# Converting float64 weights in four passes in place of six, under a written-out order, in a delta-rule attention and low-rank mixer kernel

## The chip, the core and the metric

The kernel runs on one core of a Trainium2 chip. The metric is the device time of one execution in microseconds (us). Five engines run side by side, each through its own instruction queue in program order: PE (TensorE, matmuls and transposes into PSUM), DVE (VectorE), ACT (ScalarE), POOL (GpSimd) and SP (SyncE, which here issues transfers only). An instruction waits in its queue until the results that it needs are there, and holds everything behind it in that queue.

## The reference

```python
# attention: B=4, H=8, S=768, D=48
k_n = k / (norm(k) + 1e-6)
for t in range(S):
    y[:, :, t] = q_t @ state
    state = state + beta_t * outer(k_t, v_t - state^T k_t)
x = y as (B, S, 384)
# mixer: U (768,32), V (32,768), w_ch1 (384,1536), w_ch2 (1536,384)
u = x + ((x^T @ U) @ V)^T
out = u + relu(u @ w_ch1) @ w_ch2
```

U, V and the two channel matrices are made with float64 arithmetic and reach the kernel as float64: two 32-bit words an element. q, k, v and beta are float32.

## The kernel before

**The work.** The delta rule is cut into chunks of 64 tokens. A *unit* is one batch entry and half of its sequence (six chunks, all eight heads), so there are eight units, n = 0 to 7. For each unit the kernel loads k, q and v (L518), transposes k and q on PE (L633, copied out by ACT at L647), forms the products of keys (L660), lays their diagonal blocks out on DVE with a long transpose (L736), takes the norms (sqrt on ACT, L580), and inverts the 32x32 blocks on DVE by substitution, column by column (L745 and L751, a serial chain of up to 62 instructions). A second long transpose (L758) brings the result back, and small matmuls join the blocks (L801 to L862, with copies on ACT at L806, L849, L868, L880). Then the recurrence over chunks runs: PE, then DVE (L1022), PE, then DVE (L1047), with the outputs copied to X on ACT (L908). For each batch entry the mixer follows: `front` (L1335 to L1381: the product with U, with V, and a transpose), `channels` (L1438, the first channel matrix, Relu on ACT at L1403) and `narrow` (L1553, the second one in seven products, summed into X on DVE at L1478). The last batch entry's first channel matrix uses L1238 instead.

**The weights.** There are 14 slices, i = 0 to 13: U (192 elements in each of 128 partitions), V, six slices of w_ch1 and six of w_ch2 (768 elements in each partition). SP (POOL for U) issues their transfers as pairs of 32-bit words (L1119) into three rooms: part of X, a tile `wide`, and part of `hs`; by turns 0 1 0 1 2 0 1 2 0 1 0 1 0 1. A room is loaded again when its slice is `freed`. DVE and ACT make float32 of the words: DVE cuts out the exponent (L1142) and the upper mantissa (L1148) of the high word, adds the low word scaled by 2^-32 (L1154); ACT turns the exponent field into a power of two with a Relu (L1127); DVE puts the sign on (L1160) and multiplies mantissa by power into the weight tile (L1170). `freed` follows L1160. `front` needs U and V, `channels` y needs slice 2+y, `narrow` needs the slices from 8 on and sums of them (L1077).

**The order.** Nothing is ordered by hand in the loops. Every piece of work is a Python generator that yields `op(engine, cost, ...)` before each instruction and `need(...)` for what must come first. `run()` is a list scheduler: it keeps an estimated clock for each engine, and among the pieces that could start soon takes the one with the lowest *place*, a priority from the text table `PLACES`. What comes out is one fixed instruction order for each engine, and it is this order that the chip sees. PSUM is handed out in four pairs of banks (`take`, `give`) in the same order.

Of the kernel before, what the change touches and what calls it, by code (L numbers as in the profile page):

```python
# [10 lines left out]
U32 = mybir.dt.uint32  # L11
ALU = mybir.AluOpType
# [14 lines left out]
def kernel(  # L27
# [60 lines left out]
    asked, missing, awaited, woken, quads = {}, {}, {}, [], set()  # L88
# [11 lines left out]
    def op(  # L100
        engine, cost, mode=None, take=None, give=(), lat=None, rush=None, words=0, port=None, flow=None,
        after=(),
    ):
        return dict(
            after=after,
            flow=cost * 0.95 if flow is None else flow,
            e=engine, cost=cost, mode=mode, take=take, give=give, words=words + 0.4,
            port=engine == "pool" if port is None else port,
            rush=bool(give) if rush is None else rush, lat=LAT[engine] if lat is None else lat,
        )  # L110
# [31 lines left out]
    PLACES = """  # L142
    add_up b0 i0 79; add_up b0 i1 13.98; add_up b0 i2 2.35; add_up b1 i0 40.18; add_up b1 i1 36.03
    add_up b1 i2 41.5; add_up b2 i0 77.22; add_up b2 i1 83.5; add_up b2 i2 138.32; add_up b3 i0 49.5
    add_up b3 i1 70.77; add_up b3 i2 2.5; blocks n0 2.5; blocks n1 56.67; blocks n2 -4.99; blocks n4 112
    blocks n5 123.28; blocks n7 190.8; both -10; channels b0 i0 e1 50.01; channels b0 i0 e2 94.8
    channels b0 i0 e3 -11; channels b0 i0 e4 53; channels b0 i0 e5 48.96; channels b0 i1 e2 82.12
    channels b0 i1 e4 1.27; channels b0 i1 e5 7.7; channels b0 i2 e0 93.45; channels b0 i2 e1 -29.76
    channels b0 i2 e2 41; channels b0 i2 e3 54.83; channels b0 i2 e4 220.13; channels b0 i2 e5 120.58
    channels b1 i0 e0 95.14; channels b1 i0 e1 90.59; channels b1 i0 e2 2.6; channels b1 i0 e3 20.5  # L150
    channels b1 i0 e5 75.93; channels b1 i1 e1 82.72; channels b1 i1 e3 38.5; channels b1 i1 e4 95.89
    channels b1 i1 e5 84.94; channels b1 i2 e1 -0.77; channels b1 i2 e2 88.03; channels b1 i2 e3 2.65
    channels b1 i2 e4 106.63; channels b1 i2 e5 105.76; channels b2 i0 e0 98.76; channels b2 i0 e1 100
    channels b2 i0 e3 103.94; channels b2 i0 e4 54.62; channels b2 i0 e5 101.37; channels b2 i1 e0 71.97
    channels b2 i1 e1 110.54; channels b2 i1 e2 -17.79; channels b2 i1 e4 38.5; channels b2 i1 e5 83.8
    channels b2 i2 e0 79.5; channels b2 i2 e1 148.8; channels b2 i2 e2 23.18; channels b2 i2 e3 74.5
    channels b2 i2 e4 94.46; channels b2 i2 e5 96.7; diagonals n0 h0 42.32; diagonals n0 h1 70.57
    diagonals n1 h0 2.5; diagonals n1 h1 76.19; diagonals n2 h0 18.79; diagonals n2 h1 98.94
    diagonals n3 h0 78.08; diagonals n3 h1 69; diagonals n4 h0 67; diagonals n4 h1 21.77; diagonals n5 h0 31.5
    diagonals n5 h1 8.5; diagonals n6 h0 40.59; diagonals n6 h1 104; diagonals n7 h0 8.5; diagonals n7 h1 74.99  # L160
    first 126.7; first_of_last 96.5; front b0 i0 94.5; front b0 i2 73.04; front b1 i0 80.34; front b1 i1 76.11
    front b1 i2 123.31; front b2 i0 66.93; front b2 i1 98.32; front b2 i2 -8.5; front b3 i1 101; front b3 i2 34.14
    gather b0 i0 h0 c0 42.82; gather b0 i0 h1 c0 104.34; gather b0 i0 h1 c1 36.58; gather b0 i1 h0 c0 67.77
    gather b0 i1 h0 c1 63; gather b0 i1 h1 c0 88; gather b0 i1 h1 c1 -32.01; gather b0 i2 h0 c0 87.83
    gather b0 i2 h0 c1 38; gather b0 i2 h1 c0 151.77; gather b0 i2 h1 c1 56.81; gather b1 i0 h0 c0 -21.78
    gather b1 i0 h1 c1 69.02; gather b1 i1 h0 c0 112.22; gather b1 i1 h0 c1 3; gather b1 i1 h1 c1 4.54
    gather b1 i2 h0 c0 58.39; gather b1 i2 h0 c1 -1; gather b1 i2 h1 c0 21.95; gather b1 i2 h1 c1 32
    gather b2 i0 h0 c0 7.28; gather b2 i0 h0 c1 76.31; gather b2 i0 h1 c1 62.25; gather b2 i1 h1 c0 53.05
    gather b2 i1 h1 c1 98.26; gather b2 i2 h0 c0 26; gather b2 i2 h1 c0 69.29; gather b2 i2 h1 c1 68.5
    gather b3 i0 h0 c1 -14.78; gather b3 i0 h1 c0 115; gather b3 i0 h1 c1 80.5; gather b3 i1 h0 c0 41.85  # L170
    gather b3 i1 h0 c1 33.5; gather b3 i1 h1 c0 -6.5; gather b3 i1 h1 c1 102; gather b3 i2 h0 c0 75.5
    gather b3 i2 h1 c0 6.38; gather b3 i2 h1 c1 -23.64; grams n0 i1 32.5; grams n1 i0 53.5; grams n1 i1 110.77
    grams n2 i0 20; grams n2 i1 17; grams n3 i0 28.59; grams n3 i1 9.78; grams n4 i0 77.18; grams n5 i0 131.89
    grams n5 i1 107.96; grams n6 i1 -2.5; grams n7 i0 111.34; grams n7 i1 62.06; joins n0 h0 2.01
# [125 lines left out]
    def start_of(i, s):  # L300
        e, was = s["e"], last.get(i)
        at = max(was[1] if was and was[0] == e else ready[i], clock[e])
        if s["port"]:
            at = max(at, clock["port"])
# [1327 lines left out]
```

## Time and profile before

| | us |
|---|---|
| runs | 614.04, 616.64, 616.75 |
| median | 616.64 |
| span of the profiled execution (first to last instruction) | 611.9 |
| PE busy in the span | 574.0 |
| DVE busy | 417.7 |
| ACT busy | 235.0 |
| POOL busy | 97.9 |

The profile records one execution, and its span is the only time listed for it; the median run is 4.7 us longer than that span. Busy times of PE are those of pipelined matmuls, so an engine that reads as fully busy is not at its peak. The profile also gives the granted clock of TensorE, as a share of full speed, in each stretch of time. Shares are averages over the span; what a change in one stage is worth is read from that stage.

### The profile page before, as it was taken

What the parts mean: (1) busy time and instruction counts of PE and PEld (TensorE: products, weight loads), DVE (VectorE), ACT (ScalarE), POOL (GpSimd) and SP (SyncE); (2) the same over time, 40 slices, a digit from 0 to 9 for tenths busy, and PEclk for the clock granted to TensorE, in tenths of its full rate; (3) what the DMA queues carried; (4) which work ended last, traced back from release to release, by engine and by line L of the source; (5) the groups of instructions that cost most, each with busy time, mean ns of one, the idle gap of its engine ahead of it and who ended that gap; (6) DMA issues with size and microseconds to landing.
All of it is one profiled execution on the core that took longest, in us unless ns stands there. A gap on an engine that the chain in (4) does not pass through costs nothing.

```text
span 611.9 us, 23481 instructions
## 1 busy us (share of the span) xinstructions
PE 574.0 (94%) x10548; PEld 493.7 (81%) x10548; DVE 417.7 (68%) x1000; ACT 235.0 (38%) x462; POOL 97.9 (16%) x169
## 2 busy tenths in 40 slices
PE   3697968899999999999999999999999999999997
PEld 3596867688889888789898988789889868656997
DVE  4999998998989328998896068898872135232542
ACT  2575665446322553245124451354243221344000
POOL 9221112611141104101003214010100000000000
PEclk9767575999999999999999999999999999999999
DMA  9721659920152104300002315100200000000000
GB/s 153 145 48 56 209 173 188 181 64 4 43 107 38 47 4 80 72 14 3 29 0 51 78 42 93 36 1 3 67 3 2 29 3 1 26 0 1 16 37 27
DMA packets 63845, 33.28 MB, mean 54 GB/s; under 512 B 50816, under 2 KB 61824, under 8 KB 63744
## 3 DMA queue, kind: packets, MB, share of 16 engines
q1 hardware_dynamic: 56800, 23.21, 17.6%
q0 software_dynamic: 5344, 8.27, 6.4%
q8 instruction: 83, 1.36, 0.9%
q10 hardware_dynamic: 1600, 0.30, 0.3%
q14 instruction: 18, 0.15, 0.1%
HBM read 27.03 MB, written 4.72 MB: 52 GB/s over the span
## 4 chain that ended last, share of the span: by engine, by line
PE 78%; DVE 13%; ACT 2%; issue 2%; DVEq 0%; ACTq 0%
PE P L1553 27%; PE P L1438 23%; PE P L1238 7%; PE P L660 2%; PE P L1009 2%; PE P L633 2%; PE P L924 2%; PE P L1037 1%; PE P L938 1%; DVE prod L745 1%; DVE xt L751 1%; PE P L960 1%; PE P L971 1%; PE P L1378 1%; PE P L1335 1%
## 5 line engine op out<-in xcount | busy, mean ns | idle before, releaser
L1438 PE MATMUL P<-ut,w_sb 128*128 128x256 f32 x648 | 152.5, 386 | 0.0
L1438 PEld LDWEIGHTS P<-ut,w_sb 128*128 128x128 f32 x648 | 119.0, 190 | 18.9 <-issue 1.8
L1553 PE MATMUL P<-w_sb,hs 128*128 128x192 f32 x540 | 94.6, 330 | 0.2 <-ACT hs L1403 0.2
L1553 PEld LDWEIGHTS P<-w_sb,hs 128*128 128x128 f32 x540 | 87.5, 190 | 3.6 <-issue 1.2
L1478 DVE TENSOR_TENSOR X<-X,P 128x192 f32<-128x192 f32 x84 | 29.5, 351 | 59.6 <-PE P L1553 59.0
L751 DVE TENSOR_TENSOR xt<-xt,prod 128x112 f32<-128x112 f32 (+21 forms) x200 | 64.6, 323 | 6.9
L745 DVE TENSOR_TENSOR prod<-gs,xt 128x112 f32<-128x112 f32 (+21 forms) x200 | 64.1, 320 | 4.8
L1403 ACT ACTIVATE hs<-P 128x512 f32<-128x512 f32 x54 | 32.3, 598 | 85.5 <-PE P L1438 74.4
L908 ACT COPY X<-P 64x192 f32<-64x192 f32 x96 | 30.1, 314 | 63.1 <-PE P L938 62.1
L1553 PE MATMUL P<-w_sb,S 128*128 128x192 f32 x288 | 50.7, 330 | 0.0
L1553 PEld LDWEIGHTS P<-w_sb,S 128*128 128x128 f32 x288 | 46.6, 190 | 1.2 <-DVE X L1478 0.6
L633 PE MATMUL P<-ident,slot 128*128 128x128 f32 x192 | 30.5, 313 | 15.9 <-DMA slot<-in_k_dram 10.3
L633 PEld LDWEIGHTS P<-ident,slot 128*128 128x128 f32 x192 | 25.8, 162 | 18.2 <-issue 10.9
L647 ACT COPY slot<-P 128x768 f32<-128x768 f32 x30 | 23.1, 802 | 45.0 <-PE P L633 44.8
L518 POOL DMA_DIRECT2D slot<-in_k_dram x44 | 28.9, 664 | 50.7 <-PE P L1037 50.1
L880 ACT COPY slot<-zz 32x384 f32<-32x384 f32 x64 | 32.3, 508 | 8.7 <-DVE zz L758 6.5
L518 POOL DMA_DIRECT2D slot<-in_v_dram x32 | 21.0, 663 | 90.5 <-PE P L633 89.6
L660 PE MATMUL P<-slot 48*64 48x64 f32 x1536 | 32.3, 240 | 2.2 <-ACT slot L647 2.2
L1238 PE MATMUL P<-slot,w_sb 128*128 128x384 f32 x96 | 33.3, 486 | 0.0
L1022 DVE TENSOR_TENSOR z<-slot,P 128x192 f32<-128x192 f32 x44 | 15.5, 352 | 25.6 <-PE P L1009 25.1
L660 PEld LDWEIGHTS P<-slot 48*64 48x64 f32 x1536 | 29.3, 153 | 4.3 <-ACT slot L647 3.2
L1553 PE MATMUL P<-w_sb,slot 128*128 128x192 f32 x180 | 30.6, 327 | 0.9 <-DVE X L1478 0.9
(143 smaller groups left out, 889.5 us busy)
## 6 DMA issues: line engine op xcount, KB each, us to landing
out_dram<-X SPq DMA_DIRECT2D x22, 192.0 KB, 1.8
X<-in_moe_w_ch_dram SPq DMA_DIRECT2D x10, 384.0 KB, 4.5
wide<-in_moe_w_ch_dram SPq DMA_DIRECT2D x10, 384.0 KB, 4.5
slot<-in_k_dram SPq DMA_DIRECT2D x48, 72.0 KB, 5.0
slot<-in_k_dram POOLq DMA_DIRECT2D x44, 72.0 KB, 5.0
slot<-in_q_dram POOLq DMA_DIRECT2D x32, 72.0 KB, 4.8
slot<-in_q_dram SPq DMA_DIRECT2D x32, 72.0 KB, 5.4
slot<-in_v_dram SPq DMA_DIRECT2D x32, 72.0 KB, 3.3
```

Of the source, the lines that this page charges most:

```text
L518: queue.dma_start(out=t[half(1 - g if name == "z" else g), :, to, 0:D], in_=src[b, 4 * g + s, hf * UC * L : (hf + 1) * UC * L, :].rearrang ...
L633: nc.tensor.transpose(p_t[:, c // 3, c % 3], t[:, c, 2 * j : 2 * j + 2].rearrange("p s d -> p (s d)"), ident,)
L660: nc.tensor.matmul(p_g[half(g ^ (par * i)), par, c], kq[rows, c, j, 0, half(g)], kq[rows, c, j, i, half(g)], start=True, stop=True,)
L745: nc.vector.tensor_tensor(out=prod, in0=gb[:, :, j : j + 1, j + 1 :].to_broadcast([128, split, m, w]), in1=xb[:, :, 0:m, j : j + 1].to_bro ...
L751: nc.vector.tensor_tensor(out=xb[:, :, 0:m, j + 1 :], in0=xb[:, :, 0:m, j + 1 :], in1=prod, op=ALU.subtract,)
L880: nc.scalar.copy(pg[quarter(i), :, at, :, a : a + BK], cut(zc, h)[quarter(i)].rearrange("p r (c j) t -> p r c j t", j=2),)
L908: nc.scalar.copy(x[half(c % 2), c // 2, 4 * D * g : 4 * D * (g + 1)].rearrange("p (j r d) -> p r j d", r=2, d=D), states(p_y)[half(g)],)
L1238: nc.tensor.matmul(to, w, t, start=start, stop=stop, skip_group_check=True)
L1403: nc.scalar.activation(hs[:, fs[0] : fs[1] + 1 : fs[1] - fs[0]], p_f, ACTF.Relu)
L1438: nc.tensor.matmul(p_f[:, x], w(x, t), ut[:, t], start=(t == 0), stop=(t == KT - 1))
L1478: nc.vector.tensor_tensor(out=to, in0=to, in1=p, op=ALU.add)
L1553: nc.tensor.matmul(to, of[0], of[1], start=of[2], stop=of[3], skip_group_check=True)
```

## The change

Two things change together.

**The conversion.** ACT now reads the high words where they landed, as if they were float32, and multiplies them by 2^-112 into one of two scratch tiles (even and odd slices). DVE shifts the result left by three bits into the weight tile, puts the sign of the high word on, and adds the low word, scaled by 2^-29 and rounded, to the lower 16-bit half of each element in place. So a slice takes one ACT and three DVE instructions where it took one and five, and ACT's comes first. ACT's instruction waits for the transfer, and `freed` follows the last DVE instruction.

**The order.** `PLACES` and the scheduler go. A table `ORDER` lists, for 2,139 steps, which generator goes on next; `run()` follows it. The costs in `op(...)` no longer decide anything. Some waits are added that any order has to keep (for instance, a store of an output row waits until all four of its sums are in). PSUM banks go to the longest-free pair. No matmul is added or removed.

```diff
-    PLACES = """
-    add_up b0 i0 79; add_up b0 i1 13.98; add_up b0 i2 2.35; add_up b1 i0 40.18; add_up b1 i1 36.03
...
+    ORDER = """
...
     def run():
-        stall, forms = {}, {}
-        while waits or woken:
...
+        wake()
+        for y in range(len(ORDER)):
+            i = ORDER[y]
+            s, got = waits[i], None
+            s = s[0] if isinstance(s, tuple) else s
             if s["take"]:
...
-        uppers, powers = room[:, 2 * WIDE :], exponents
+        scaled = [t.bitcast(FP32) for t in (room[:, 2 * WIDE :], exponents)]
...
-        def raised(i, power):
-            cost = 0.16 + size(i) * 0.001
-            yield op("act", cost)
-            nc.scalar.activation(
-                power, power, ACTF.Relu, bias=bias_e, scale=2.0 ** 23
-            )
-            emitted(("raised", i))
+        def raised(i):
+            yield need(("wide", i), ("shifted", i - 2))
+            yield op("act", act(size(i)))
+            high = landed[i][:, :, 1].bitcast(FP32)
+            nc.scalar.mul(shape(i, scaled[i % 2][:, 0 : size(i)]), shape(i, high), 2.0 ** -112)
+            emitted(("raised", i), 0.06)
...
-            nc.vector.tensor_scalar(
-                out=power, in0=h, scalar1=20, scalar2=0x7FF,
-                op0=ALU.logical_shift_right, op1=ALU.bitwise_and,
-            )
-            begin(raised(i, power), 39)
-            nc.vector.tensor_scalar(
-                out=upper, in0=h, scalar1=0x000FFFFF, scalar2=0x00100000,
-                op0=ALU.bitwise_and, op1=ALU.bitwise_or,
+            nc.vector.tensor_single_scalar(
+                out=bits, in_=shape(i, scaled[i % 2][:, 0:n]).bitcast(I32), scalar=3,
+                op=ALU.logical_shift_left,
             )
-            mant = upper.bitcast(FP32)
             nc.vector.scalar_tensor_tensor(
-                out=mant, in0=low, scalar=2.0 ** -32, in1=upper,
-                op0=ALU.mult, op1=ALU.add,
-            )
-            yield need(("raised", i))
-            nc.vector.scalar_tensor_tensor(
-                out=power, in0=h, scalar=-(1 << 31), in1=power,
+                out=bits, in0=h, scalar=-(1 << 31), in1=bits,
                 op0=ALU.bitwise_and, op1=ALU.bitwise_or,
             )
-            emitted(("freed", i))
+            halves_of = dst.bitcast(U16)
+            tail = halves_of[..., 0::2]
             nc.vector.scalar_tensor_tensor(
-                out=dst, in0=mant, scalar=2.0 ** -20, in1=power, op0=ALU.mult, op1=ALU.mult
+                out=tail, in0=low.bitcast(U32), scalar=2.0 ** -29, in1=tail,
+                op0=ALU.mult, op1=ALU.add,
             )
+            emitted(("freed", i))
             emitted(("weights", i), 0.1)
```

What the written-out order does to the queues, as far as the prediction speaks of it. SP's first four transfers are half of unit 0's k (before, they were unit 1's, and unit 0's came fifth to eighth). U's transfer is POOL's first (before, it came after 14 others), and U's conversion stands among the first products of unit 0 on ACT and DVE. V's four transfers are spread over SP's first twenty (before, they came after twenty). The sqrt that ran on ACT once at the very start (L529) stands in the middle of the program, and the load of ACT's function table that went with it now stands in front of unit 0's norms (L580). Apart from that the stages follow one another as before.

More of the change, by code (lines that the diff above doesn't have):

```diff
@@ L148 @@
[L148 to L152, printed above, removed]
@@ L158 @@
[L158 to L162, printed above, removed]
@@ L380, in run @@
             for tag, x in s["give"]:
-                free[tag][x] = state["now"] + s["lat"]
-            last[i] = s["e"], state["now"]
-            advance(i, got, state["now"] + s["lat"])
+                free[tag][x] = state["now"]
+            advance(i, got, state["now"])
+            wake()
+        assert not waits
     def pair(x):
```

513 lines of the change are left out of this document (272 added, 241 removed).

## Prediction

> **What bounds the kernel now.** I read the page's totals, then its slices, then cut the span at the long transposes of VectorE, then looked inside the stage that this shows.
>
> ```profile
> span 611.9 us, 23481 instructions
> ...
> PE 574.0 (94%) x10548; PEld 493.7 (81%) x10548; DVE 417.7 (68%) x1000; ACT 235.0 (38%) x462; POOL 97.9 (16%) x169
> ...
> PE   3697968899999999999999999999999999999997
> ...
> DVE  4999998998989328998896068898872135232542
> ...
> PEclk9767575999999999999999999999999999999999
> ...
> PE 78%; DVE 13%; ACT 2%; issue 2%; DVEq 0%; ACTq 0%
> ```
>
> TensorE is the bound, but not everywhere: it has holes and a clock below full only in the first eight slices, some 120 us, and there VectorE is full. Where the stages begin and end (first column start, second length):
>
> ```profile
> 15.77 1.94 DVE L736 STREAM_TRANSPOSE gs<-slot 128x1024 f32<-128x1024 f32 x1
> ...
> 34.00 1.91 DVE L736 STREAM_TRANSPOSE gs<-slot 128x1024 f32<-128x1024 f32 x1
> ...
> 53.34 1.96 DVE L758 STREAM_TRANSPOSE zz<-xt 128x1024 f32<-128x1024 f32 x1
> ...
> 110.69 2.02 DVE L736 STREAM_TRANSPOSE gs<-slot 128x1024 f32<-128x1024 f32 x1
> ```
>
> These are unit 0's layout, unit 1's, the end of unit 1's substitution, and unit 2's layout. Busy time by stage, cut there and at 148.8 (the sums of the weights); the columns are length, PE, PEld, DVE, ACT, POOL, granted clock, DMA share, GB/s:
>
> ```profile
> 0.00:9.90 9.90, 0.01 (x1) 0.04 (x1) 3.94 (x21) 1.49 (x2) 9.09 (x23) 1.00 0.92 135
> 9.90:15.80 5.90, 5.50 (x136) 5.04 (x137) 2.59 (x7) 2.22 (x5) 5.71 (x9) 1.00 1.28 182
> 15.80:34.00 18.20, 12.85 (x245) 11.46 (x245) 16.84 (x50) 11.53 (x23) 5.36 (x9) 0.72 0.68 129
> 34.00:53.30 19.30, 18.84 (x684) 17.59 (x680) 17.86 (x54) 12.45 (x27) 3.29 (x7) 0.65 0.13 32
> 53.30:110.70 57.40, 46.10 (x1425) 42.06 (x1428) 53.34 (x92) 34.15 (x67) 11.17 (x19) 0.61 0.65 176
> 110.70:148.80 38.10, 35.81 (x842) 28.57 (x838) 35.00 (x74) 18.53 (x33) 10.59 (x18) 1.00 0.48 85
> 148.80:611.90 463.10, 454.92 (x7235) 388.99 (x7226) 288.11 (x707) 154.60 (x308) 52.70 (x88) 1.00 0.15 32
> ```
>
> From 53.3 to 110.7 VectorE is busy 53.34 of 57.40 us and TensorE 46.10: VectorE is the bound, TensorE is idle for 11.3 us and runs at 0.61 of its clock. After 148.8 TensorE is idle for 8.2 us in 463.1. So whatever VectorE saves before 110.7 can shorten the run; what it saves after that can win little.
>
> **The change part by part.** *A slice.* One slice of 768 elements, as VectorE does it now:
>
> ```profile
> 79.14 0.55 DVE L1142 TENSOR_SCALAR power<-X 128x768 int32<-128x768 int32 x1
> 79.61 0.55 DVE L1148 TENSOR_SCALAR X<-X 128x768 int32<-128x768 int32 x1
> 80.20 0.96 DVE L1154 SCALAR_TENSOR_TENSOR X<-X 128x768 f32<-128x768 uint32 x1
> 81.08 0.95 DVE L1160 SCALAR_TENSOR_TENSOR power<-X,power 128x768 int32<-128x768 int32 x1
> 82.06 0.96 DVE L1170 SCALAR_TENSOR_TENSOR w_sb<-X,power 128x768 f32<-128x768 f32 x1
> ```
>
> That is 3.88 us from 79.14 to 83.02. The new shift is L1142's kind (one source, one operation on integers): 0.47, from start to start. The new sign is L1160's: 0.98. The rounded low half, with 16-bit elements two apart, is not in the trace; its ends are 0.55 (L1148, the shortest row of this length) and 1.94 (L736, the longest near it); I take L1170's 0.98, because that has the same two sources and one result. Together 2.43, so 1.45 a slice; 13 long slices give 18.9 and U, a quarter as long, some 0.5: **19.4 us less on VectorE**. At 1.94 for the low half it would be 7.
>
> ScalarE's pass stays one a slice:
>
> ```profile
> L1127 ACT ACTIVATE power<-power,bias_e 128x768 int32<-128x768 int32 x13 | 12.2, 938 | 6.8 <-DVE power L1142 6.6
> ```
>
> Its new form reads words 8 bytes apart. I take 0.94 again; ScalarE is busy 34.15 of 57.40 us in the stage, so a tenth more or less costs nothing there.
>
> *The start.* TensorE's first work waits for unit 0's k:
>
> ```profile
> 9.89 2.79 PE L633 MATMUL P<-ident,slot 128*128 128x128 f32 x12 [9.89 <-DMA slot<-in_k_dram]
> ...
> L518 SPq DMA_DIRECT2D slot<-in_k_dram x12: 596/624/723, 0.8 to 8.5; - x12
> ...
> L529 ACT ACT_TABLE_LOAD x1 | 1.3, 1283 | 3.9 <-issue 3.9
> ...
> X<-in_moe_U_dram POOLq DMA_DIRECT2D x1, 192.0 KB, 7.1
> ```
>
> SP issues that half of k four places earlier, at 0.624 us each: 2.5 us less. Against it: U's three passes, on a quarter of the elements, some 0.9 us, now stand on VectorE among unit 0's first products, and they wait for a transfer that took 7.1 us to land; issued at about 4, it lands by 8 to 11, when TensorE's first results are about ready, so up to 1.5 us of waiting. And the table load that ran at 3.9 beside the wait for k now stands in front of unit 0's sqrt, with VectorE's long transpose (1.94) to hide it: 0 to 1.28, I take 0.6. Net: -1.0, between -2.5 and +1.5.
>
> [...]
>
> *Units 0 and 1 (15.8 to 53.3).* By the changed program's instruction order VectorE has the same work between these marks, but for this: from L736 to L736 two masks (L691) and one L767 less, by the rows below 2 x 0.55 + 0.57 = -1.7; from L736 to L758 three passes of V, two of slice 2 and one L767 more, three of U fewer, 2.43 + 1.45 + 0.57 - 0.9 = +3.6. VectorE is busy 34.7 of 37.5 us there, so both count in full: +1.9.
>
> ```profile
> L691 DVE TENSOR_TENSOR slot<-P,mask_u 128x384 f32<-128x384 f32 x16 | 8.3, 546 | 0.3 <-PE P L660 0.3
> ...
> L767 DVE STREAM_TRANSPOSE zz<-zz 128x384 f32<-128x384 f32 x12 | 6.7, 570 | 0.5
> ```
>
> *The long stage (53.3 to 110.7).* In it stand 54 passes now (the last two of U, five of V, five each of slices 2 to 10, two of slice 11): 0.7 + 3.9 + 9 x 3.88 + 1.0 = 40.5 us. In the new order 26 stand there (one of slice 2, three each of 3 to 10, the shift of 11): 1.0 + 8 x 2.43 + 0.5 = 20.9. Two masks come in, 1.1. VectorE's work falls by 18.5, from 53.3 to 34.8 us. Then VectorE is no longer the bound: TensorE's 46.10 is. With all of its 11.3 us of waiting gone the stage takes **46.1 us, 11.3 less**; with VectorE alone in charge, and the 4.1 us that it now waits kept, 38.9.
>
> Which of the two depends on the clock. TensorE in windows of 3.4 us (length, busy, clock, DMA share, GB/s):
>
> ```profile
> 63.60:67.00 3.40, 3.40 (x117) 0.50 0.85 282
> 67.00:70.50 3.50, 3.50 (x117) 0.50 0.78 237
> ...
> 84.10:87.50 3.40, 2.21 (x121) 0.97 0.60 192
> ```
>
> Two windows busy from end to end stay at 0.50, and one at two thirds of that gets 0.97: with these small tiles a denser stream does not by itself raise the clock. So I keep 46.1.
>
> [...]
>
> *After 110.7.* To 148.8 VectorE's list is shorter still (the last slices take 1.45 less each, and some work of unit 2 falls outside), and TensorE is idle for 2.3 us: I take 1.0 of it as won, between 0 and 2.3. After 148.8 TensorE's own order is almost the old one: the stages follow each other within a few us of its work, and mode changes and matmuls are as many. I take 0, between -3 and +4.
>
> *The sum.* -1.0 + 1.9 - 11.3 - 1.0 = **-11.4 us**. The profiled span would become 600.5. Around it lie 4.7 us to the median of the runs (616.64, from 614.04 to 616.75), so the median becomes **605.2**. A measurement of this kernel can tell about 0.5%, 3.1 us, from no change.
>
> **The rivals.**
>
> [...]
>
> *VectorE's passes were only filling.* The recurrence goes PE, VectorE, PE, VectorE, twelve times, and its delays, not VectorE's load, set the long stage; then it stays near 55 and the run near 614. For it: the stage's clock is low. Against: VectorE is 93% busy there, and its recurrence steps stand in one queue behind passes of 0.96 us.
>
> *The transfers take over.* ScalarE's pass now waits for the transfer itself, and the room is freed only by the last pass:
>
> ```profile
> X<-in_moe_w_ch_dram SPq DMA_DIRECT2D x10, 384.0 KB, 4.5
> ...
> SPq L1119 <- DVE power L1160: 30.0, 6, 12.4
> ...
> L1142 DVE TENSOR_SCALAR power<-X 128x768 int32<-128x768 int32 x5 | 2.9, 573 | 0.4 <-DMA X<-in_moe_w_ch_dram 0.4
> ```
>
> Now SP waits for VectorE (30.0 us), and VectorE hardly for transfers (0.4). One turn of a room becomes two issues (1.2), landing (4.5), ScalarE (0.94), VectorE (2.43): 9.1 us; rooms 0 and 1 make three and two or three turns in the long stage, so 28 us fit. With turns of 15 (landings near 10, since the DMA share is already 0.65) the stage is 47 us and nothing more is won: 606.
>
> *Slower: the fixed order starves TensorE after 148.8.* It has 8.2 us of idle in 463.1. The order places each unit's joins and recurrence at fixed points among `channels` and `narrow`; if the substitution on VectorE isn't through when TensorE's queue gets to the joins, everything behind them waits. Units 3 to 7 make five such places. At 3 us each the 11.4 are more than used up; at 5 it is 25 and the run takes 630. Against it: from 148.8 on VectorE is 62% busy, and its list reaches each unit's layout some 20 us of its own work earlier than before, while TensorE's does not move.
>
> **How the numbers follow.** The forecast, with its neighbours from 601 to 609 (the transfers included): 0.55. The clock comes up: 0.22. Passes were only filling: 0.12. Slower: 0.11. The range should hold 8 in 10: from 596, the clock's rival with 1 us to spare, to 613, which leaves out most of the filling case (614) and the slow case. Faster by over 0.5% (below 613.5): 0.55 + 0.22 + half of the filling case = 0.83. Within 0.5%: the other half, 0.06. Slower: 0.11.
>
> **What would show it.** Right: the passes at about 0.5, 0.95 and 0.95 us; TensorE's first work near 7; the second L736 to L758 about 2 us longer; 46 us for the long stage with TensorE 95% busy at a clock near 0.6; the same 463 us after. [...]

## The result, and the profile after

Times in us; a ratio is the changed kernel's to that of the kernel before in runs on the same chip.

| | before | after | ratio (95% interval) |
|---|---|---|---|
| first set, 20 runs each | 616.44 | 613.94 (610.00 to 619.22) | 0.995 (0.9932 to 0.9967) |
| second set | 616.17 | 614.57 (610.45 to 619.41) | 0.9982 (0.9956 to 1.0009) |

So by the medians the change gains 1.6 to 2.5 us where 11.4 were forecast (the interval of the second set reaches 1, so there the gain is not clear of noise), and the median lies just above the forecast's range (596 to 613). The profiled execution of the first set took 617.97, 4.0 more than the median of its set, so its span is read stage by stage and not against the median.

The page of the changed kernel: totals, three rows of the 40 slices, the chain by engine.

```profile
span 616.3 us, 23450 instructions
...
PE 581.1 (94%) x10548; PEld 499.2 (81%) x10548; DVE 393.1 (64%) x971; ACT 232.4 (38%) x463; POOL 96.5 (16%) x169
...
PE   5598986899999999999999999999999999999997
...
DVE  5878684688689616989697248998774124224352
...
PEclk9955555789999999999999999999999999999999
...
PE 84%; DVE 7%; DMA 3%; ACT 2%; issue 2%; POOL 1%; SPq 0%; DVEq 0%; ACTq 0%; POOLq 0%
```

VectorE has lost 24.6 us of work (417.7 to 393.1) and is no longer full in the first eight slices. TensorE has not filled up in its place, and DMA, which the page listed with no share in the chain before, has 3% of it.

The groups of the four passes, by line (busy us, mean ns, idle before), agree with the forecast's prices but for two small terms: the shift takes 0.56 us where 0.47 was taken, and the low half, which had no row before, 1.02 to 1.04 where 0.98 was taken:

```profile
L1157 DVE TENSOR_SCALAR w_sb<-power 128x768 int32<-128x768 int32 x6 | 3.3, 558 | 6.1 <-ACT power L1143 6.1
...
L1164 DVE SCALAR_TENSOR_TENSOR w_sb<-X,w_sb 128x768 int32<-128x768 int32 x5 | 4.8, 956 | 0.1
L1171 DVE SCALAR_TENSOR_TENSOR w_sb<-hs,w_sb 128x768 uint16<-128x768 uint32 x2 | 2.1, 1042 | 0.0
```

```profile
L1143 ACT ACTIVATE power<-wide 128x768 f32<-128x768 f32 x5 | 4.5, 899 | 6.5 <-DMA wide<-in_moe_w_ch_dram 6.4
```

The stages, cut at the same long transposes as before (lines are L742 for the layouts, L764 for the way back): first unit 0's layout to unit 1's, then to the end of unit 1's substitution, then the long stage, then the rest. Columns: length, PE, PEld, DVE, ACT, POOL, granted clock, DMA share, GB/s.

```profile
14.24:31.78 17.54, 9.37 (x212) 8.14 (x212) 14.98 (x46) 11.56 (x21) 3.65 (x6) 0.89 0.95 168
31.78:56.66 24.88, 22.54 (x625) 21.09 (x625) 20.41 (x58) 14.90 (x29) 6.68 (x12) 0.50 0.40 102
56.66:112.89 56.23, 46.51 (x1496) 42.80 (x1490) 36.29 (x67) 30.83 (x62) 11.84 (x20) 0.56 0.55 137
112.89:616.26 503.38, 495.43 (x8107) 420.86 (x8104) 313.99 (x776) 171.45 (x346) 62.72 (x107) 0.99 0.16 36
```

In the long stage VectorE's work fell by 17.0 us (53.34 to 36.29; 18.5 forecast) and the stage by 1.2. VectorE now idles for 19.9 us there, and TensorE still waits for 9.7 (56.23 less 46.51). What they waited for in that stage (us in total, times, longest):

```profile
ACT power L1143 <- DMA wide<-in_moe_w_ch_dram: 6.4, 2, 3.8
...
DVE w_sb L1157 <- ACT power L1143: 5.0, 3, 2.3
PE P L1020 <- DVE s L1059: 3.6, 4, 2.3
...
ACT X L1143 <- DMA X<-in_moe_w_ch_dram: 2.2, 2, 1.5
```

That reads as a chain: the transfer of a slice is late, ScalarE's pass waits for it, VectorE's shift waits for ScalarE, the recurrence's L1059 stands behind the shift, and TensorE waits for the state. In the chain of work that ended last, cut at 84 to 106 us, two whole landings of slices (start, length) make 12.7 us:

```profile
87.79 6.28 DMA wide<-in_moe_w_ch_dram
...
98.90 6.38 DMA wide<-in_moe_w_ch_dram
```

This chain was the first theory, **theory 1** (called A later): the waits of passes placed ahead of their transfers. **Theory 2** was that TensorE at half its clock sets the stage and VectorE's passes were only filling; **theory 3** that the written-out order costs what the conversion wins.

### The profile page after: what moved, and what is told of

It is laid out like the page before. It is cut to its first block, busy times and chain, and to the rows that moved or that the text cites. A ratio compares the mean times of both kernels' runs of the same rounds, so it can differ in the third digit from the quotient of the medians.

```text
span 616.3 us, 23450 instructions
## 1 busy us (share of the span) xinstructions
PE 581.1 (94%) x10548; PEld 499.2 (81%) x10548; DVE 393.1 (64%) x971; ACT 232.4 (38%) x463; POOL 96.5 (16%) x169
## 3 DMA queue, kind: packets, MB, share of 16 engines
q8 instruction: 83, 1.36, 0.9%
## 4 chain that ended last, share of the span: by engine, by line
PE 84%; DVE 7%; DMA 3%; ACT 2%; issue 2%; POOL 1%; SPq 0%; DVEq 0%; ACTq 0%; POOLq 0%
PE P L1562 28%; PE P L1442 22%; PE P L1241 7%; PE P L666 3%; PE P L639 3%; DMA wide<-in_moe_w_ch_dram 2%; PE P L1020 2%; PE P L971 2%; DVE xt L757 2%; PE P L982 2%; DVE prod L751 2%; PE P L945 2%; PE P L808 2%; PE P L1048 2%; PE P L822 2%
## 5 line engine op out<-in xcount | busy, mean ns | idle before, releaser
L1562 PE MATMUL P<-w_sb,hs 128*128 128x192 f32 x540 | 96.0, 331 | 0.0
L1562 PEld LDWEIGHTS P<-w_sb,S 128*128 128x128 f32 x288 | 46.6, 190 | 2.2 <-issue 1.2
L666 PE MATMUL P<-slot 48*64 48x64 f32 x1536 | 33.7, 241 | 6.1 <-ACT slot L653 4.9
L887 ACT COPY slot<-zz 32x384 f32<-32x384 f32 x64 | 32.4, 508 | 13.6 <-DVE zz L764 11.6
```

The lines of the kernel that those rows point to most:

```text
L666: nc.tensor.matmul(p_g[half(g ^ (par * i)), par, c], kq[rows, c, j, 0, half(g)], kq[rows, c, j, i, half(g)], start=True, stop=True,)
L887: nc.scalar.copy(pg[quarter(i), :, at, :, a : a + BK], cut(zc, h)[quarter(i)].rearrange("p r (c j) t -> p r c j t", j=2),)
L1562: nc.tensor.matmul(to, of[0], of[1], start=of[2], stop=of[3], skip_group_check=True)
```

## The experiments

All eighteen at a glance, beside the kernel before and the changed kernel. The long stage is that between the second L764 and the third L742 (by the numbers of the changed kernel) in the one profiled execution of each; "issue" is the time that TensorE's matmuls waited in it for nothing that the profile shows. A ratio is to the kernel before on the same chip (its medians were 615.9 to 616.8); where nothing else is said, the base is the changed kernel.

| run | median | ratio (95% interval) | long stage | PE busy, clock | issue |
|---|---|---|---|---|---|
| before | 616.2 to 616.8 | 1 | 57.4 | 46.1, 0.61 | 0 |
| after | 613.94 | 0.9950 (0.9932 to 0.9967) | 56.2 | 46.5, 0.56 | 0.7 |
| after_again | 614.57 | 0.9982 (0.9956 to 1.0009) | 53.9 | 45.7, 0.58 | 0 |
| conv_only | 708.10 | 1.1489 (1.1453 to 1.1525) | 63.3 | 48.0, 0.59 | 0 |
| order_only | 619.26 | 1.0061 (1.0041 to 1.0082) | 60.9 | 46.9, 0.56 | 0 |
| no_late_loads | 606.45 | 0.9857 (0.9833 to 0.9880) | 48.4 | 41.0, 0.68 | 0 |
| later | 615.00 | 0.9980 (0.9962 to 0.9999) | 53.7 | 42.2, 0.68 | 3.9 |
| early | 612.30 | 0.9936 (0.9912 to 0.9959) | 55.1 | 44.4, 0.62 | 5.5 |
| conv_old_order | 619.91 | 1.0066 (1.0048 to 1.0085) | 60.0 | 46.6, 0.60 | 5.3 |
| filled16 | 639.46 | 1.0384 (1.0356 to 1.0412) | 74.7 | 70.3, 0.55 | 0 |
| no_late_passes | 614.86 | 0.9994 (0.9971 to 1.0017) | 56.6 | 45.6, 0.58 | 5.8 |
| no_late_either | 609.53 | 0.9888 (0.9862 to 0.9914) | 49.6 | 43.3, 0.63 | 0.8 |
| early_warm | 613.72 | 0.9953 (0.9930 to 0.9975) | 52.6 | 43.3, 0.64 | 1.9 |
| split | 612.55 | 0.9932 (0.9906 to 0.9958) | 53.4 | 40.6, 0.71 | 0 |
| shifted_fetch | 617.67 | 1.0016 (0.9995 to 1.0037) | 58.6 | 46.9, 0.58 | 6.8 |
| split_later | 613.99 | 0.9971 (0.9954 to 0.9989) | 53.8 | 44.8, 0.66 | 0.2 |
| split_later_warm | 613.08 | 0.9948 (0.9930 to 0.9966) | 53.3 | 43.7, 0.65 | 0 |
| conv_old_split | 618.15 | 1.0037 (1.0018 to 1.0056) | 57.6 | 45.9, 0.64 | 3.7 |
| shifted_half | 620.57 | 1.0078 (1.0051 to 1.0104) | 56.9 | 42.4, 0.66 | 8.3 |
| before_no_late | 616.46 | 0.9992 (0.9974 to 1.0010) | 56.9 | 46.0, 0.61 | 0.6 |

### A second profile

> The changed kernel once more, unaltered, for a second profile: the first profiled execution (617.97 us) was one of its longest, against a median of 613.94. Every theory expects 613 to 615 for the median. If the stage between the end of unit 1's substitution and unit 2's layout was long by chance in that execution, it will be below 53 us here (it was 56.2) and units 0 and 1 below 22 us (24.9); if what holds it is built into the order, both come out within 2 us of the first profile.

The stage of units 0 and 1 came out the same to 0.01 us (24.87), the long stage 2.3 us shorter than in the first profile: above the 53 us that chance would have given, and a little outside the 2 us of the other reading:

```profile
31.61:56.48 24.87, 22.60 (x628) 21.07 (x626) 20.36 (x57) 15.56 (x30) 6.68 (x12) 0.54 0.42 102
56.48:110.41 53.93, 45.70 (x1482) 42.10 (x1482) 36.21 (x66) 30.29 (x60) 11.57 (x20) 0.58 0.56 142
```

From here on this profile stands for the changed kernel: 8.2 us of TensorE waiting in the long stage.

### Each part alone

```diff
 # conv_only: the kernel before, its scheduler and places, with the new raised() and load_weights()
 # order_only: the changed kernel with, for each slice,
+            nc.vector.tensor_scalar(out=power, in0=high, scalar1=20, scalar2=0x7FF, ...)
+            nc.scalar.activation(power, power, ACTF.Relu, bias=bias_e, scale=2.0 ** 23)
...
 # conv_old_order: the kernel before, its scheduler's picks written out as a list; in it
 #   cut of the exponent -> ScalarE's pass; 3rd, 4th, 5th VectorE step -> shift, sign, low half
```

> The new conversion alone, in the order that the old scheduler and its places make of it. Transfers (theory 1: ScalarE's pass now waits for its slice and holds the recurrence behind it on ScalarE and VectorE): 611 to 615, with ScalarE waiting over 4 us for transfers of the weights between 53 and 111 us. Clock (theory 2: TensorE at half its clock sets that stage, and VectorE's passes were only filling): 613 to 617, stage of 54 to 57 us at a clock near 0.55 and little waiting for transfers. The written order loses what the conversion wins (theory 3): 604 to 608, stage of 46 to 49 us.

708.1 us, outside all three. The scheduler's places no longer fit the costs and waits that it sees: its order loses most of the time after the long stage (120.5 to 703.1, TensorE idle for 63.6 us there). It says nothing of the conversion; conv_old_order replaces it.

> The written-out order alone, with the old arithmetic of the conversion in it: five VectorE instructions a slice (two before and mantissa times power before the sign, so that the scratch tile comes free in time), ScalarE's Relu. VectorE has about 17 us more to do in the long stage than in the changed kernel. Theory 1 (transfers): the exponent's cut now waits for each slice on VectorE itself and the recurrence behind it, 618 to 626. Theory 2 (clock; VectorE's passes were filling): within 3 us of the changed kernel, 612 to 617. Theory 3 (the written order costs): 619 or more, with after 148 us no difference to the changed kernel.

619.26, 3.1 slower than before and 4.7 slower than the changed kernel: theory 2, which gave 612 to 617, falls for a VectorE that is this busy (47.8 of 60.9 us), theory 3 holds so far. Its engines waited for transfers of weights for only 0.9 us, so theory 1's reason isn't the one.

> The new conversion alone, in the very instruction order of the kernel before, written out step by step: ScalarE's pass stands where the exponent was cut out, the shift in the place of the third VectorE instruction, sign and low half in those of the fourth and fifth; a room's next transfer is issued up to three steps later, because the room comes free one pass later. VectorE loses the same 19 us as in the changed kernel. Theory 1 (each pass waits for its transfer on an engine in order): 611 to 615 with ScalarE waiting over 4 us for transfers in the long stage. Theory 3 (the written order costs what the conversion wins; by the order alone it costs 3): 606 to 610, with a long stage of 46 to 50 us. If the two parts simply add (order +3.1, both -1.6): 611 to 612.

619.91: slower than before by 0.5 to 0.9%, which none of the three had, so theory 3, by which 606 to 610 was due, falls too. VectorE's work in the long stage fell by 13.4 us (53.33 to 39.90) and the stage grew by 2.6. ScalarE waits for transfers for only 2.0 us; TensorE waits 5.3 us in it "for issue", that is for no other engine:

```profile
53.55:113.53 59.98, 46.60 (x1424) 42.63 (x1428) 39.90 (x70) 34.51 (x68) 12.09 (x20) 0.60 0.65 167
```

```profile
PE P L1214 <- issue: 3.4, 2, 2.7
```

So each part alone is 3 us worse and both together 2 us better: they don't add.

### The late transfers

```diff
-                queue.dma_start(out=to, in_=of)
+                if i < 8:
+                    queue.dma_start(out=to, in_=of)
```

> The changed kernel without the transfers of slices 8 to 13 (the second channel matrix is left out and whatever stood in the rooms is converted in its place), all passes kept. Theory 1 (transfers): the waits of ScalarE for the rooms' transfers (6.4 + 2.2 us between 50 and 125 us in the first profile) and the recurrence's waits behind them go, stage of 56 down to 48 to 51 us, 606 to 609. Theory 2 (clock): TensorE at 0.5 to 0.6 of its clock still needs the time, 612 to 614, stage 54 to 56. Theory 3 (order): as theory 2.

606.45, as theory 1 had it (606 to 609), stage 48.4; 7.4 us of TensorE's waiting are left:

```profile
56.29:104.65 48.36, 40.97 (x1482) 37.36 (x1482) 35.88 (x66) 30.47 (x62) 11.43 (x19) 0.68 0.35 84
```

This run takes away two things at once: that anything waits for these transfers, and their traffic. The runs without passes, further on, part them. This one also shows something that the waits alone don't: against the second profile of the changed kernel the stage is 5.6 us shorter, but only 0.8 of that is waiting (8.2 to 7.4). The other 4.7 is TensorE's own busy time on the same 1,482 matmuls (45.70 to 40.97): the 176 of L1020 took 301 ns each there and 278 here, and the granted clock is 0.58 and 0.68. Why TensorE runs faster without these transfers is not shown.

```diff
 # later: ORDER, old step -> new place
-raised i9: 399; its passes: 400 405 414; start i11: 427; raised i10: 428; its passes: 432 435 444; raised i11: 441
+raised i9: 418; its passes: 420 424 430; start i11: 430; raised i10: 455; its passes: 457 459 462; raised i11: 490
 # (and the shift of i11: 449 -> 500)
 # early: start i9 (second half): 382 -> ahead of 381, the load of unit 2's k
```

> The changed kernel with eleven of its 2,139 steps moved back: ScalarE's pass and VectorE's three of slices 9 and 10, ScalarE's pass of 11 and VectorE's shift of it, by some 15 to 50 steps each, and the issues of slice 11 with them. No work and no transfer is added or left out. Theory 1 (passes placed ahead of their transfers hold the recurrence on ScalarE and VectorE): ScalarE's waits for these transfers (3.7 + 2.0 + 0.8 us in the second profile) fall under 2 us in all, the stage from 53.9 to 48 to 50 us, the run to 608 to 611. If the transfers matter by their traffic and not by where they are waited for: no change, 613 to 615. Theory 2 (half clock): no change, 613 to 615.

615.00: theory 1's 608 to 611 fell. The waits for the weights did go (1.1 us left of 6.6), but the stage stayed at 53.7: TensorE was busy for 3.5 us less and waited for 3.4 more (11.6). In place of the waits for the weights stands waiting of its own that the changed kernel's second profile did not have:

```profile
PE P L679 <- issue: 1.5, 1, 1.5
PE P L944 <- issue: 1.4, 1, 1.4
...
PE P L995 <- issue: 1.0, 1, 1.0
```

> The changed kernel with one step moved: on SP, the second half of slice 9's transfer goes ahead of the first transfer of unit 2's k, behind which it stood (that k waits for unit 0's recurrence). Theory 1: slice 9 lands 1 to 1.5 us sooner, ScalarE waits for it some 2.3 us instead of 3.7, and the run gains 1 to 1.5 us: 612.5 to 613.5. Theory 2, or transfers that share one bandwidth: no change, 613 to 615.

612.30, just below what theory 1 gave, though its profile doesn't show the gain in the long stage (55.1, with 5.5 us for issue); its interval overlaps that of the changed kernel, so it tells nothing apart.

### Filling TensorE

```diff
+            if s["e"] == "pe" and 40 <= y < 485 and s["mode"]:
+                nc.tensor.matmul(P[:, 7, 384:512], ident16, ident16, start=True, stop=True, ...)
```

> The changed kernel with some 120 small extra matmuls on TensorE (128 x 128 times 128 x 128 in 16-bit floats, into a part of PSUM that nothing reads), one before each of its pieces of work from about 20 to 110 us, to make the array denser. Theory 2 (half clock sets the stage): the granted clock there rises from 0.54 and 0.58 to over 0.8, units 0 and 1 and the long stage shorten by 5 us or more together, run 605 to 610. Theory 1 (waits behind transfers): the clock may rise, the stage's waits stay, 612 to 618. If the clock doesn't rise, the extra matmuls cost at most 0.1 to 0.2 us each where TensorE is busy: 615 to 630.

639.46, worse than all three. (With them the kernel no longer computes the reference; it is read for its times.) Each took 0.2 to 0.3 us. In the long stage TensorE was busy for 70.3 of 74.7 us at a granted clock of 0.55, and in these 3.4 us windows, busy from end to end, it stayed at half its clock:

```profile
37.80:41.20 3.40, 3.40 (x66) 0.50 0.02 5
41.20:44.60 3.40, 3.40 (x53) 0.50 0.46 108
44.60:48.00 3.40, 3.40 (x82) 0.50 0.59 163
```

So a denser stream of such matmuls did not bring the clock up, as the forecast had it from its two windows.

### Traffic without anyone waiting for it

```diff
 # no_late_passes; no_late_either has `if i < 8` at the transfers too
+            if i < 8:
                 nc.scalar.mul(...)           # and so VectorE's shift, sign and low half
+    nc.vector.memset(w2_sb[:, 0:4].rearrange("p a f d -> p (a f d)"), 0.5)
```

> The changed kernel with the transfers of slices 8 to 13 kept, but ScalarE's pass and VectorE's three passes of them left out (the second channel matrix is a constant that VectorE writes at the start, some 4 us of work beside the first transfers), so that no engine waits for these transfers. Theory A (passes in order wait for transfers, and the recurrence behind them): the long stage, 53.9 us in the second profile of the changed kernel, comes down to 46 to 49 us. Theory B (the traffic itself holds TensorE up: its instructions come by transfers too, 83 of some 16.4 KB in the page's third part, and the earlier run with the passes moved back had 3.9 us of TensorE waiting for issue where the run without the transfers had none): 51 to 54 us, with TensorE waiting 3 us or more for issue.

> As the run before, and the transfers of slices 8 to 13 left out too. Both theories: 45 to 48 us for the long stage and under 2 us of TensorE waiting for issue. Against the run without the transfers but with the passes (48.4 us): what the passes of slices 8 to 10 (7.7 us of VectorE) still cost, 0 to 3 us. If the stage stays above 51 us, neither passes nor transfers set it.

The windows of the long stage, first with the transfers, then without:

```profile
56.82:113.39 56.57, 45.55 (x1482) 41.60 (x1482) 28.85 (x56) 26.99 (x56) 11.54 (x20) 0.58 0.56 136
```

```profile
56.76:106.33 49.57, 43.25 (x1482) 39.59 (x1482) 28.78 (x56) 26.89 (x56) 11.54 (x20) 0.63 0.35 84
```

Theory A falls as the whole cause. With the transfers and nobody waiting for them the stage takes 56.6 us, longer than B's 51 to 54, and the run 614.86; without them 49.6 and 609.53. TensorE's waits for issue make 5.8 and 0.8 us: 5 of the 7. The rest is its own work at a somewhat lower clock (45.55 us at 0.58 and 43.25 at 0.63). VectorE is busy for 51 and 58% of the stage. Against no_late_loads, leaving out the passes wins nothing (49.6 with 48.4): once VectorE is below TensorE, its passes cost nothing here.

### What TensorE waits for

The page counts a queue of 83 transfers, 1.36 MB, so 16.4 KB each; TensorE has 10,548 matmuls and as many weight loads, 254 to each of them:

```profile
q8 instruction: 83, 1.36, 0.9%
```

If these are its instructions, a wait must stand at every 128th matmul and move when matmuls are put ahead.

```diff
+            if y == 6:
+                for _ in range(64):          # 32 in shifted_half
+                    nc.tensor.matmul(P[0:32, 7, 384:416], ident[0:32, 0:32], ident[0:32, 0:32], ...)
```

> The run without the passes of slices 8 to 13 but with their transfers, with 64 matmuls of 32 x 32 more on TensorE at the very start, while it waits for k. In that run TensorE waited for issue 0.91, 0.75 and 4.12 us ahead of its recorded matmuls 2270, 2411 and 2564, some 147 apart. If these are waits for TensorE's instructions (83 transfers of 16.4 KB, 256 instructions of 64 bytes each by the counts of the page, so one for each 128 matmuls and weight loads), 64 pairs ahead of them move each boundary back by half such a piece: waits of 0.5 us or more near the old numbers 2200, 2340 and 2490, on other lines, and none at the old places. If the waits belong to those matmuls (a bank, a transfer of data, a mode), they stay at the same lines, L983, L932 and L946 by the old numbers.

The waits stayed, which by itself spoke for the other reading. But each matmul in the source had become two (10,676 on the page), so the shift was 128 pairs, a whole piece, and the page shows 84 transfers. Half of it was then tried:

> As the run with the 64 small matmuls at the start, with 32. Each of those 64 came out as two matmuls and two weight loads (10,676 recorded on the page in place of 10,548, and 84 instruction transfers in place of 83): together one whole piece of 256 instructions, and the two longest waits for issue stood at the same places as without them, one matmul ahead of the end of a group of 16 (L932 by the old numbers) and two ahead of the end of another (L946). With 32 the shift is half a piece. If the waits are for TensorE's instructions, they leave those two places and stand some 64 matmuls away from them, that is four groups of 16 earlier. If they belong to those matmuls, they stay.

The end of the long stage on TensorE in no_late_passes (start, length, instruction, count, wait), then in shifted_half, where L952 is the old L946 and L938 the old L932:

```profile
94.30 0.66 PE L932 MATMUL P<-s,slot 48*64 48x48 f32 x15
95.71 0.34 PE L932 MATMUL P<-s,slot 48*64 48x48 f32 x1 [0.75 <-issue]
...
99.73 0.67 PE L946 MATMUL P<-z,slot 64*64 64x48 f32 x14
104.52 0.45 PE L946 MATMUL P<-z,slot 64*64 64x48 f32 x2 [4.12 <-issue]
```

```profile
91.24 0.41 PE L952 MATMUL P<-z,slot 64*64 64x48 f32 x15
95.00 0.20 PE L952 MATMUL P<-z,slot 64*64 64x48 f32 x1 [3.34 <-issue]
...
99.22 0.67 PE L938 MATMUL P<-s,slot 48*64 48x48 f32 x14
104.58 0.24 PE L938 MATMUL P<-s,slot 48*64 48x48 f32 x1 [4.68 <-issue]
```

The waits fall inside groups of 16 equal matmuls, where no result is awaited. In both kernels 127 recorded matmuls lie between the two waits. And in program order each wait of shifted_half stands exactly four groups, 64 matmuls, ahead of its place in no_late_passes. So **TensorE waits for its own instructions**, which come by transfer in pieces of some 256 (127 recorded matmuls and their weight loads from wait to wait, 254 to a transfer on the page) and come late while the weights are on their way (5.8 us of such waiting in no_late_passes, 0.8 in no_late_either). One wait took up to 4.68 us.

The scheduler that the change takes out had a term of this kind: `late()` in its source counts TensorE's instruction words in lots of 256 (`LOT`) and holds a lot back, longer when transfers are queued. So the order before was chosen with it in the sum; the prediction did not take it up.

### Pieces, and the parts together

```diff
-                queue.dma_start(out=to, in_=of)
+                for x in range(3) if kind == "a" else range(2):     # the channel matrices
+                    queue.dma_start(out=to[:, x], in_=of[:, x])
 # early_warm: early, and the sqrt of step 750 at step 9; split_later: split and later; _warm: that sqrt too
 # conv_old_split: conv_old_order and split
```

> The changed kernel with each half-slice transfer of the two channel matrices issued as three pieces (first matrix) or two (second), nothing else changed. Theory B (instruction fetch behind large transfers): fetches get in between, TensorE's clock and work unchanged, 609 to 612. Theory A: two to four more issues of 0.6 us on SP make each slice land later, 614 to 618. If neither: 613 to 615.

612.55, and no wait for issue on the matmuls at all. But TensorE now waits 6.5 us for the state, because ScalarE waits 8.0 us for the slices: one wait for the other.

> The changed kernel with two steps moved: the second half of slice 9's transfer ahead of unit 2's k (as in the run that gave 612.3), and the small sqrt that brings ScalarE's function table moved from the middle of the program to the start, beside the wait for k. The table load (1.28 us ahead of unit 0's norm at 16 us) goes: unit 1's layout, the second long transpose, comes 1.0 to 1.3 us sooner after the first (17.25 us in the second profile of the changed kernel), run 610.5 to 611.5. If VectorE's other work at that place is the later, nothing changes: 612 to 613.

The table load was worth 1.0 us, as expected (16.28 us from layout to layout, against 17.25 in after_again; the sqrt starts within 0.02 us of the load's end in the first profile), but the run (608.71 to 619.62, median 613.72) is no faster than early.

> The two changes together, each of which the earlier runs had alone: transfers of the channel matrices issued in two or three pieces each (no waits for issue there, but 6.5 us of TensorE waiting for the recurrence's state) and the passes of slices 9 to 11 moved back (no waits for transfers, but 3.9 us for issue). If transfers cost in both these ways at once, waits of both kinds go: long stage 47 to 50 us, run 607 to 610. If there is a third hold behind them, 52 to 54 us and 612 to 615.

> The run before with the sqrt that loads ScalarE's table moved to the start as well. From first to second long transpose of the layouts 16.3 us instead of 17.2 to 17.9, as in the run with that step moved: 1 us less than the run before, 606 to 609 if the long stage comes down to 47 to 50, 611 to 614 if it doesn't.

613.99 and 613.08: there is a third hold. Both waits are gone in split_later (0.2 us for issue, 0.7 for weights), and the stage is 53.75 us all the same. Its chain of waits, by line, runs mostly through transfers, the passes that free the rooms, and SP's queue, up to unit 2's q, and little through TensorE:

```profile
by line: DMA X<-in_moe_w_ch_dram 16.6%; DVE w_sb L1188 12.6%; SPq L1148 11.4%; DVE w_sb L1181 10.3%; SPq L537 5.1%; issue 4.8%; DMA slot<-in_q_dram 4.4%; DMA wide<-in_moe_w_ch_dram 4.1%; PE P L821 3.1%; PE P L835 2.9%; PE P L984 2.8%; DVE s
```

> The new conversion in the old order (619.91, long stage 59.98 us with 5.3 us of TensorE waiting for issue), with the transfers of the channel matrices issued in two or three pieces. If the waits for issue are what made that run slower than the kernel before, they go here: stage 53 to 56, run 613 to 616. If the pieces help only under the new order: 618 to 621.

618.15: the pieces bring 1.8 us in the old order, the waits for issue fall from 5.3 to 3.7 only, and the run stays above the kernel before. That the fetches alone make conv_old_order slower is not shown.

No version clearly beats the changed kernel: split (0.9932), early (0.9936) and the changed kernel (0.995 and 0.998) have intervals that overlap.

### Where the gain went

> The kernel before, without the transfers of slices 8 to 13 (the second channel matrix is left out and whatever stood in the rooms is converted in its place), all six passes kept; beside it stands the changed kernel without the same transfers, 606.45 us, long stage 48.4. If VectorE's passes are what bounds the kernel before, as the forecast had it, the transfers cost it nothing: long stage 55 to 57.4 us, run 613 to 616.5, and without the transfers the change is worth 7 to 10 us. If the transfers hold the kernel before up as much as the changed one: stage 49 to 52, run 608 to 611, and the change is worth 2 to 4 us either way.

616.46, the time of the kernel before, and VectorE still full in the long stage:

```profile
57.14:114.05 56.91, 45.97 (x1424) 41.91 (x1428) 53.16 (x92) 34.10 (x67) 11.01 (x19) 0.61 0.44 113
```

Without the late transfers the change is worth 616.46 less 606.45, **10.0 us** by the medians, which come from two chips, and 8.3 by the ratios to the kernel before on each chip (0.9992 less 0.9857); with them 1.6 to 2.5. The kernel before loses nothing to the transfers (616.46 without them, 616.79 with them on that chip); VectorE is busy for 53 us of its long stage either way. The changed kernel loses 7.5 to 8.1 (613.94 and 614.57 less 606.45).

How the 8.5 us of the long stage (56.91 to 48.36) are won matters for the forecast: TensorE's waiting falls by only 3.5 us (10.9 to 7.4), and its busy time by 5.0 (45.97 to 40.97) while the granted clock goes from 0.61 to 0.68.

## Why the prediction was wrong, step by step

The terms below compare single profiles. That of the kernel before is a short execution (span 611.9, where one of the median time spans some 614.7), the first of the changed kernel a long one (616.3, median some 612.2); together the terms give +4.4 where the medians give -1.6 to -2.5. Each is good to a few us.

- *The conversion's price:* right. 0.56, 0.95 and 1.03 us a slice; the rows of the passes add up to 53.2 us before and 33.8 after, the 19.4 less that were forecast. VectorE's busy time fell by 24.6 in all and by 17.0 in the long stage (18.5).
- *The start:* -1.5 for -1.0 (unit 0's layout at 14.24 for 15.77), but not by the forecast's parts: TensorE's first work came at 5.29 us, where "near 7" was expected, and then waited 1.63 us for the other half of k. The kernel before itself had this layout at 15.77 and, in before_no_late, 17.88, so the sum's agreement is in part luck. The table load cost 1.0 where 0.6 was taken, and it falls behind this mark, into the next term.
- *Units 0 and 1:* the sign right, the reason not: +4.9 for +1.9 (42.42 us for 37.57). The forecast had VectorE's work grow by 1.9; it grew by 0.7 (34.70 to 35.39), and the rest is waiting. In the second profile these are two waits of VectorE for the joins of unit 0 (2.0 and 1.3 us) and one for the norms (1.1), which the sum over VectorE's list could not show. From the second layout on, that stage took 24.86 to 24.90 us in twelve of the thirteen profiles of the new order with the new conversion (filled16 apart), whatever was done after it.
- *The long stage:* **here it failed**, in the words "with all of its 11.3 us of waiting gone the stage takes 46.1 us". TensorE's busy time was right (46.5, 45.7). The waiting fell to 9.7 and 8.2 us instead of to none. The step went from "VectorE is no longer the bound" to "TensorE is", and two things stand against it. It left out the third resource in that stage, the transfers: without the late ones the stage takes 48.4 us, with them 56.2 and 53.9. They hold it up in ways that take each other's place: passes in order wait for a slice (8.0 us of ScalarE in split), instructions come late (5.8 us of TensorE in no_late_passes), and rooms turn slowly (12.0 us for one turn in the second profile). And it put at nothing the waits that TensorE has for results even then: 7.4 us of waiting stay without the late transfers, the largest share (2.9) before L1020, which waits for the recurrence's L1059. That the forecast for a kernel without these transfers would have been near (46.1 for 48.4 us in the stage, 11.4 for 8.3 to 10.0 in all) is luck: with TensorE's busy time as forecast and that waiting the stage would have been some 53.5, and what made up for it was TensorE's shorter busy time at a higher clock (40.97 us at 0.68, before 46.1 at 0.61), which is something of "the clock comes up".
- *After the long stage:* -1.0 forecast; the rest is 2.0 and 2.2 us longer in the two profiles. In the other eleven profiles of this order and conversion, with and without the late transfers, it took 498.7 to 505.0 us (501.2 before), so single profiles don't tell this term.
- *The rivals.* "The clock comes up", which has 0.22 of the chances and gives the range its lower end (596), was an estimate: no run shows a denser stream raising the clock. It read 0.56 and 0.58 in the long stage of the changed kernel (before 0.61), 0.55 in that of filled16, where TensorE was busy for 70.3 of 74.7 us, and no long stage was shorter than 48.4 us, where 38.9 was put down for VectorE alone in charge. "Passes were only filling" came nearest to the time (614). That the recurrence's delays alone keep the stage near 55 is refuted, since without the late transfers the lighter passes shorten it by 8.5 us (56.9 to 48.4); that its delays remain when VectorE has room is right (the 7.4 us above). "The transfers take over" named the right resource with the wrong price: one room turn, put at 9.1 us, was 12.0 in the second profile (slice 9's room free at 85.4, slice loaded by 93.4, free again at 97.4), and it did not have the instruction fetch at all. It put the run at 606; with the full 8 us that the transfers cost, its place was 614. "Slower" didn't happen: TensorE is idle for 6.3 us after 150.3, where the kernel before had 8.2 after 148.8.

Open: why the pieces of split let the instructions through, how the share of 5 us for instructions in no_late_passes divides in the changed kernel itself (its first profile shows 0.7 us of waiting for issue, its second none), why TensorE's own time is shorter without the late transfers, and why both parts alone are slower.

## What to carry over

When an engine is relieved in a stage, list everything else that is dense in that stage, the transfers and their share of time included, and what the next engine still has to wait for, before giving the whole of its waiting to the gain; a wait that vanishes can uncover the next one that ran beside it (in later the waits for weights fell from 6.6 to 1.1 us, and 3.9 us for issue came in). Two kernels, one that leaves the transfers out and one that leaves out what waits for them, tell a late result from traffic at little cost; compare the busy times in them as well as the waits. Waits "for issue" at even distances in a long unrolled stream (here 127 recorded matmuls) are worth counting in instructions.

## What the runs showed of the hardware

- TensorE's instructions come by transfers of 16.4 KB, one for each 128 matmuls and weight loads (by the counts of the page, 83 transfers for 10,548 of each, and by the 127 recorded matmuls from wait to wait). In long stages with 130 to 170 GB/s of transfers on average TensorE waited up to 4.68 us for one of them (shifted_half); with the transfers issued in pieces of 128 and 192 KB in place of 384 hardly any such wait (0.2 us at most in the long stage) was seen under the new order.
- The granted clock of a window can mislead. In later it reads 1.00 for the stage of units 0 and 1 from the second layout on, in after_again 0.54, and the same matmuls took the same time in both (mean ns after the comma):

```profile
L679 PE MATMUL P<-slot 48*64 48x64 f32 x144 | 5.3, 316 | 0.1
```

```profile
L666 PE MATMUL P<-slot 48*64 48x64 f32 x144 | 5.6, 317 | 0.1
```

Durations of one shape are the better witness: the same form takes 220 ns between 250 and 400 us in after_again, where the clock reads 1.00 too.
- A pass over 768 elements with 16-bit results two apart took 1.02 to 1.04 us, hardly more than one with whole words (0.95); ScalarE's pass over words 8 bytes apart took 0.90 to 0.93, no more than the old one over words in a row (0.94).
